# Two inner loops swapped around the 32 small matmuls that form a chunk's state increments

## The chip, the cores and the metric

The kernel runs on one core of one Trainium2 chip. The metric is the device time of one execution in microseconds (us), as the median of several runs. The profile is of one further execution.

## What is computed

A gated linear recurrence over the sequence, per batch and head, followed by a two-layer network with a PReLU between the layers. Everything is float32.

```python
B, H, S, D = 4, 8, 768, 48
f = sigmoid(f_logit)
for t in range(S):
    state = f[:, :, t, :, None] * state + outer(k[:, :, t], v[:, :, t])   # per batch, head: D x D
    y[:, :, t] = q[:, :, t] @ state
x = y.transpose(0, 2, 1, 3).reshape(B * S, H * D)      # 3072 x 384
h = x @ w_in                                            # 384 x 2048
out = (maximum(h, 0) + alpha * minimum(h, 0)) @ w_out   # 2048 x 384
```

## The kernel before

The sequence is cut into 6 chunks of `C = 128` positions, and each chunk into `NC2 = 2` halves of `CH = 64`. Two batches (`U = 2`) are worked on together, so that there are 12 steps: for each chunk, first batches 0 and 1 (`bp = 0`), then 2 and 3 (`bp = 1`). The 8 heads stand as `HP = 4` pairs: the 48 dims of the even head of a pair (`par = 0`) on partitions 0 to 47, those of the odd head (`par = 1`) on 64 to 111. A tile that is named by its dims holds key or query dims on partitions and time along the row.

Each step has three parts, written as generators:

- `prepare` loads f, q, k and v of the chunk (`L223`, `L233`) and forms on VectorE (DVE) and ScalarE (ACT) the decayed queries and keys: products of gates within groups of four positions, scans over blocks of 32, and from these `q3`, `ks`, `kh` and `f64` (the decay over one half).
- `attend` runs the matmuls of the recurrence: `raw` (`L343`) and `qu` (`L359`) give the scores within blocks of 32 positions, `off` (`L377`) those between the two blocks of a half. `pk` (`L390`) turns the decayed keys `ks` so that time lies on partitions, and ACT copies them to `ksn` (`L393`). Then `pd` (`L406`) forms the increments of the state; this is the place of the change. `moved` (`L416` to `L421`, DVE) adds an increment to the decayed state, and `py` (`L434`) forms the outputs from state, scores and v.
- `network` runs the two layers over the 256 rows of the step: `ph` (`L464`), PReLU on ACT and DVE (`L469`, `L472`), `po` (`L480`), and the results leave from `o` (`L486`).

The increments. For batch `u`, head `2 hp + par` and half `cc`, the increment is the product of the half's decayed keys (64 positions x 64 columns, of which 48 are dims) with its values (64 positions x 48). The positions of half 0 lie on partitions 0 to 63 and those of half 1 on 64 to 127, both in `ksn` and in `vs`; so this decides the rows of TensorE's 128 x 128 array that a matmul uses. The result of half 0 goes to partitions 0 to 63 of `pd`, and that of half 1 to 64 to 127; this decides the columns. A matmul of half 0 thus uses the quarter of the array with rows and columns 0 to 63, one of half 1 the quarter with rows and columns 64 to 127. `par` and `hp` only choose other columns of the same tiles. `pd` is a pair of banks of the accumulator memory PSUM, one for each `u`. There are U x HP x NC2 x 2 = 32 of these matmuls in a step. In the profile each float32 matmul shows as two loads of its weights (LDWEIGHTS, on "PEld") and two MATMULs (on "PE").

`py` for comparison: its 32 matmuls use all 128 rows, and `par` chooses columns 0 to 63 or 64 to 127 (`L434`); `par` is its innermost loop. In `raw`, `qu` and `off`, `par` is the innermost loop too and there chooses the rows, while the next loop out chooses the columns.

The order on TensorE (PE), DVE and ACT is written by hand. The strings `first` and `usual` (`L496` to `L502`) name the generators to advance, one letter for each: S for `attend`, n for the network of the step before, Q for `prepare` of the next step, P for `prepare` of this one, w and v for the two weight matrices. In a usual step, network matmuls of the step before stand between the stages of `attend`:

```python
usual = "n S n S Q n2 Q S n2 S Q n S Q S Q n5 Q"
```

SyncE, ScalarE and GpSimd (POOL) issue the DMAs; the v of later steps comes through POOL's queue (`L233`).

Of the kernel before, what the change touches and what calls it, by code (L numbers as in the profile page):

```python
# [23 lines left out]
NC2 = C // CH  # L24
# [6 lines left out]
def kernel(  # L31
# [179 lines left out]
    def halves(cc):  # L211

        return slice(CH * cc, CH * cc + CH), slice(CH * (1 - cc), CH * (1 - cc) + D)
# [116 lines left out]
    def attend(bp, c, x):  # L330
# [68 lines left out]
        pd = pair(f"pd_{i}")  # L399
        for u in range(U):  # L400
            for hp in range(HP):
                for cc in range(NC2):
                    for par in range(2):
                        o = (2 * hp + par) * D
                        s_ = halves(cc)[0]
                        nc.tensor.matmul(pd[s_, u, o:o + D],  # L406
                                         lhsT=ksn[s_, u, hp * 128 + 64 * par:hp * 128 + 64 * par + 64],
                                         rhs=vs[bp][s_, cc, u, o:o + D], start=True, stop=True)
# [96 lines left out]
    def begin(n):  # L505
        if n >= len(steps):
            return None, None, None
        x = {}
        return [stage(*steps[n], x) for stage in (prepare, attend, network)]
# [67 lines left out]
```

## Time and profile before

| | |
|---|---|
| three runs | 691.63, 692.16, 692.86 us; median 692.16 |
| the profiled execution | 692.21 us, of which the span (first to last instruction) 690.4 |
| busy over the span | PE 638.1 us (92%), PEld 477.7 (69%), DVE 440.3 (64%), ACT 232.6 (34%), POOL 50.2 (7%) |
| chain that ended last, by engine | PE 73%, DVE 22%, ACT 2% |
| mean granted TensorE clock | 0.988 of full speed |
| `ph` matmuls (`L464`) | 1152 instructions, 267.2 us busy |
| `po` matmuls (`L480`) | 768 instructions, 251.3 us busy |

The profile is of one execution. PE is the matmul itself, PEld the load of weights, which overlaps with PE. "Busy" of an engine is the time in which at least one of its instructions ran, so instructions that overlap are counted once, while "mean ns" is the duration of a single one. The chain is followed back from the last instruction, at each step to what released it. "Idle before" is the time in which the engine stood still just ahead of the group, and what ended most of it. The ends of matmuls are modelled.

### The profile page before, as it was taken

To read this page: it belongs to the slowest core of one execution; us is meant where nothing else is said; L and a number is where in the kernel's file an instruction comes from. 1 tells how busy PE (TensorE), PEld (TensorE's weight loads), DVE (VectorE), ACT (ScalarE), POOL (GpSimd) and SP (SyncE) were. 2 spreads that over 40 slices of the span, in tenths; PEclk is the share of its full clock that TensorE was granted. 3 is DMA by queue.
4 is the path that set the end of the run, shared out by engine and by line. 5 is a ranking of instruction groups with operands and counts; after the bars stand their busy time and mean duration, and the time that the engine had idled before them with its cause. 6 is when DMAs were issued, how large, how long until landed. Compare 5 with 4: busy or idle time off the path is not lost.

```text
span 690.4 us, 16917 instructions
## 1 busy us (share of the span) xinstructions
PE 638.1 (92%) x7392; PEld 477.7 (69%) x7392; DVE 440.3 (64%) x907; ACT 232.6 (34%) x397; POOL 50.2 (7%) x89
## 2 busy tenths in 40 slices
PE   1367699999999999999999999999999999999998
PEld 0256476876876785785785786786786786786774
DVE  6998999996675693593594594495495494340120
ACT  3554573260352340440440440440440440240110
POOL 9010000010000010010010010000000000000000
PEclk9998899999999999999999999999999999999999
DMA  6656545121121220221211211121121000000000
GB/s 234 205 144 184 153 129 163 55 94 47 56 62 47 86 60 19 83 55 26 73 55 37 61 59 43 57 62 46 54 66 46 25 2 24 25 3 24 23 1 23
DMA packets 25673, 46.74 MB, mean 68 GB/s; under 512 B 3936, under 2 KB 16480, under 8 KB 25600
## 3 DMA queue, kind: packets, MB, share of 16 engines
q0 software_dynamic: 6160, 21.63, 10.9%
q1 hardware_dynamic: 13584, 21.63, 9.8%
q10 hardware_dynamic: 5856, 2.40, 1.4%
q8 instruction: 58, 0.95, 0.6%
q14 instruction: 15, 0.12, 0.1%
HBM read 36.21 MB, written 4.72 MB: 59 GB/s over the span
## 4 chain that ended last, share of the span: by engine, by line
PE 73%; DVE 22%; ACT 2%; issue 1%; DMA 1%; DVEq 0%; ACTq 0%; SPq 0%
PE po L480 33%; PE ph L464 28%; DVE ad L364 4%; PE pd L406 3%; DVE ad L350 3%; PE py L434 3%; DVE g L472 2%; PE qu L359 2%; PE pk L390 2%; PE raw L343 2%; DVE us L275 1%; DVE us L262 1%; DVE w_in_sb L189 1%; DVE w_in_sb L186 1%; PE off L377 1%
## 5 line engine op out<-in xcount | busy, mean ns | idle before, releaser
L464 PE MATMUL ph<-xT,w_in_sb 128*128 128x256 f32 x1152 | 267.2, 387 | 7.3 <-DMA xT<-y 7.3
L480 PE MATMUL po<-w_out_sb,g 128*128 128x384 f32 x768 | 251.3, 487 | 0.1
L464 PEld LDWEIGHTS ph<-xT,w_in_sb 128*128 128x128 f32 x1152 | 218.1, 193 | 43.4 <-DMA xT<-y 7.5
L480 PEld LDWEIGHTS po<-w_out_sb,g 128*128 128x128 f32 x768 | 145.3, 190 | 98.7 <-DVE w_out_sb L189 1.1
L472 DVE SCALAR_TENSOR_TENSOR g<-neg,om,ph 128x256 f32<-128x256 f32 x192 | 82.3, 476 | 193.2 <-ACT neg L469 193.0
L469 ACT ACTIVATE neg<-ph 128x512 f32<-128x512 f32 x96 | 56.9, 595 | 191.9 <-PE ph L464 115.9
L486 ACT COPY o<-po 128x384 f32<-128x384 f32 x24 | 11.5, 479 | 179.5 <-PE po L480 179.5
L364 DVE COPY_PREDICATED ad<-mquad,qu 128x224 f32<-128x224 int32 (+6 forms) x168 | 50.5, 300 | 8.0 <-DVE ad L364 0.3
L350 DVE COPY_PREDICATED ad<-mraw,raw 128x256 f32<-128x256 int32 x96 | 42.6, 444 | 11.8 <-PE raw L343 9.1
L359 PE MATMUL qu<-us,k 48*32 48x116 f32 x1536 | 28.8, 285 | 20.0 <-DVE us L275 14.1
L343 PE MATMUL raw<-qd,k 48*32 48x128 f32 x1536 | 29.3, 286 | 16.5 <-DVE qd L244 10.9
L275 DVE TENSOR_TENSOR us<-us,fs 128x768 f32<-128x768 f32 (+2 forms) x72 | 44.2, 613 | 0.1
L359 PEld LDWEIGHTS qu<-us,k 48*32 48x32 f32 x1536 | 23.5, 113 | 23.6 <-DVE us L275 14.8
L343 PEld LDWEIGHTS raw<-qd,k 48*32 48x32 f32 x1536 | 22.6, 110 | 24.4 <-issue 23.8
L326 ACT COPY A<-q 48x512 f32<-48x512 f32 x48 | 29.6, 617 | 10.3 <-DVE q L294 5.5
L397 ACT COPY A<-ad 32x512 f32<-32x512 f32 x48 | 29.5, 615 | 0.6
L406 PEld LDWEIGHTS pd<-vs,ksn 64*64 64x64 f32 x768 | 25.3, 141 | 5.7 <-issue 3.2
L244 DVE TENSOR_TENSOR qd<-qd,f 128x768 f32<-128x768 f32 (+2 forms) x36 | 27.3, 758 | 3.0 <-ACT qd L239 3.0
L434 PEld LDWEIGHTS py<-A,vs 128*64 128x64 f32 x768 | 25.0, 145 | 5.3 <-issue 4.3
L406 PE MATMUL pd<-vs,ksn 64*64 64x48 f32 x768 | 26.8, 227 | 1.2 <-ACT ksn L393 1.2
L434 PE MATMUL py<-A,vs 128*64 128x64 f32 x768 | 26.9, 231 | 0.8 <-DVE vs L416 0.8
L223 POOL DMA_DIRECT2D k<-in_kT x11 | 8.0, 727 | 255.7 <-PE raw L343 255.7
(65 smaller groups left out, 425.3 us busy)
## 6 DMA issues: line engine op xcount, KB each, us to landing
w_in_raw<-in_w_in SPq DMA_DIRECT2D x12, 511.8 KB, 4.6
w_out_raw<-in_w_out SPq DMA_DIRECT2D x12, 511.8 KB, 3.5
f<-in_fT POOLq DMA_DIRECT2D x11, 512.0 KB, 4.1
q<-in_qT POOLq DMA_DIRECT2D x11, 512.0 KB, 4.4
k<-in_kT POOLq DMA_DIRECT2D x11, 512.0 KB, 4.5
out<-o SPq DMA_DIRECT2D x24, 192.0 KB, 1.8
vs<-in_v POOLq DMA_DIRECT2D x22, 192.0 KB, 3.3
xT<-y SPq DMA_DIRECT2D x36, 48.0 KB, 3.0
```

What stands on the lines that cost most here:

```text
L275: nc.vector.tensor_tensor(us[:, :, UO[m]:UO[m] + 4 * n].rearrange("p g (i r) -> p g i r", r=4), us[:, :, skip:skip + 4 * n].rearrange("p g ...
L326: nc.scalar.copy(A[halves(cc)[1], :, par * HP:(par + 1) * HP, CH * cc:CH * (cc + 1)], q3[rows(par)].rearrange("p (u h c) s t -> p u h c (s ...
L343: nc.tensor.matmul(raw[DB * j:DB * (j + 1), par, hp * C:(hp + 1) * C], lhsT=k[r_, g:g + DB], rhs=qd[r_, 0:4 * W].rearrange("p (d x) -> p d ...
L350: nc.vector.copy_predicated(adu, mraw[:, d].rearrange("p i r -> p (i r)").bitcast(I32).unsqueeze(1).broadcast_to((128, H, DB)), rv[:, :, d])
L359: nc.tensor.matmul(qu[DB * j:DB * (j + 1), par, hp * UW:(hp + 1) * UW], lhsT=k4[r_, g * DB:(g + 1) * DB], rhs=us[r_, g], start=True, stop= ...
L364: nc.vector.copy_predicated(ad[:, u, :, :, 4 * m:DB], mquad[:, lo:lo + n].bitcast(I32).unsqueeze(1).unsqueeze(1).broadcast_to((128, 2, HP, ...
L406: nc.tensor.matmul(pd[s_, u, o:o + D], lhsT=ksn[s_, u, hp * 128 + 64 * par:hp * 128 + 64 * par + 64], rhs=vs[bp][s_, cc, u, o:o + D], star ...
L434: nc.tensor.matmul(py[64 * par:64 * par + 64, u, o:o + CH], lhsT=vs[bp][:, cc, u, hd * D:hd * D + 64], rhs=A[:, u, par * HP + hp, CH * cc: ...
L464: nc.tensor.matmul(ph[:, j * T:(j + 1) * T], lhsT=w_in_sb[:, kt, (f + j) * 128:(f + j + 1) * 128], rhs=xT[:, kt], start=(kt == 0), stop=(k ...
L469: nc.scalar.activation(neg, phv, AF.Relu, scale=-1.0)
L472: nc.vector.scalar_tensor_tensor(g[:, j], neg[:, j], om[:, f + j:f + j + 1], phv[:, j], ALU.mult, ALU.add)
L480: nc.tensor.matmul(po[u][:, 0:DM], lhsT=gs[f // 2][:, f % 2, u * C:(u + 1) * C], rhs=w_out_sb[:, f], start=(f == 0), stop=(f == NF - 1))
```

## The change

The loops over `par` and `cc` change places; `cc`, the half, is now the innermost. The body stays: the same 32 products, with the same operands and the same places in `pd`.

```diff
         for u in range(U):
             for hp in range(HP):
-                for cc in range(NC2):
-                    for par in range(2):
+                for par in range(2):
+                    for cc in range(NC2):
                         o = (2 * hp + par) * D
                         s_ = halves(cc)[0]
                         nc.tensor.matmul(pd[s_, u, o:o + D],
```

For each pair of heads the four matmuls came as half 0 even head, half 0 odd head, half 1 even head, half 1 odd head. Now they come as half 0 even, half 1 even, half 0 odd, half 1 odd. In the program of the changed kernel, the wait for the v of half 1 stands at the second matmul of a stage where it stood at the third; the order of the instructions on the other engines is the same.

## The prediction

> **What bounds the kernel now.** I read the page first: busy times, slices, the chain that ended last, the costliest groups. Then busy time by stretch, one stretch for each of the 12 chunk steps, the timeline of one step, and the single instructions of L406. The page, as columns: busy us (share of the span) and instructions; slices in tenths; shares of the chain; then groups with busy us, mean ns of one | idle before.
>
> ```profile
> span 690.4 us, 16917 instructions
> ...
> PE   1367699999999999999999999999999999999998
> ...
> PEclk9998899999999999999999999999999999999999
> ...
> PE po L480 33%; PE ph L464 28%; DVE ad L364 4%; PE pd L406 3%; DVE ad L350 3%; PE py L434 3%; DVE g L472 2%; PE qu L359 2%; PE pk L390 2%; PE raw L343 2%; DVE us L275 1%; DVE us L262 1%; DVE w_in_sb L189 1%; DVE w_in_sb L186 1%; PE off L377 1%
> ...
> L359 PE MATMUL qu<-us,k 48*32 48x116 f32 x1536 | 28.8, 285 | 20.0 <-DVE us L275 14.1
> ...
> L406 PEld LDWEIGHTS pd<-vs,ksn 64*64 64x64 f32 x768 | 25.3, 141 | 5.7 <-issue 3.2
> ...
> L434 PEld LDWEIGHTS py<-A,vs 128*64 128x64 f32 x768 | 25.0, 145 | 5.3 <-issue 4.3
> L406 PE MATMUL pd<-vs,ksn 64*64 64x48 f32 x768 | 26.8, 227 | 1.2 <-ACT ksn L393 1.2
> L434 PE MATMUL py<-A,vs 128*64 128x64 f32 x768 | 26.9, 231 | 0.8 <-DVE vs L416 0.8
> ```
>
> The reader is to see three things. TensorE (PE) is full from about the sixth slice (some 85 us) to the end. The edited line, L406, is on the chain with 3% of the span, so what it gains or loses ends up in the time. And all of L406 is 26.8 us of PE, so nothing done to it can be worth more than that. A matmul of the source shows as two loads and two matmul instructions: 12 steps x 32 matmuls = 384 in the source, 768 in the row.
>
> The steps, as stretches: length, PE busy (count), PEld busy, DVE, ACT, POOL, clock, DMA.
>
> ```profile
> 304.80:357.20 52.40, 51.98 (x618) 38.87 (x617) 33.58 (x69) 16.55 (x29) 3.38 (x5) 1.00 0.19 54
> ```
>
> PE is busy for 51.98 of 52.40 us, VectorE (DVE) for 33.58. What is saved on PE in such a step comes off the step, and the same holds for what is added. The timeline around that step's L406 and L434 (start, us of the group):
>
> ```profile
> 353.29 1.98 PEld L406 LDWEIGHTS pd<-vs,ksn 64*64 64x64 f32 x64 [0.33 <-issue]
> 353.29 2.10 PE L406 MATMUL pd<-vs,ksn 64*64 64x48 f32 x64
> ...
> 355.32 2.46 PEld L464 LDWEIGHTS ph<-xT,w_in_sb 128*128 128x128 f32 x12
> ...
> 358.11 1.95 PEld L434 LDWEIGHTS py<-A,vs 128*64 128x64 f32 x64 [0.33 <-issue]
> 358.11 2.09 PE L434 MATMUL py<-A,vs 128*64 128x64 f32 x64
> ```
>
> So one L406 stage is 64 loads in 1.98 us, 31 ns each, though one load lasts 135 ns from start to end; the work is pipelined, and what counts is the distance between starts.
>
> **The change part by part.** No instruction is added or removed, no shape changes, and no other line moves. Per stage, 32 matmuls change their order. A matmul of half 0 uses rows 0 to 63 and columns 0 to 63 of the array, one of half 1 rows and columns 64 to 127. Before, the halves come as 0 0 1 1; after, 0 1 0 1. The question is whether the two quarters worked one after the other before.
>
> *Do they overlap already?* The records of single instructions in the stage at 353.29 say yes. Loads start at 353.293, .306, .348, .361, .404, .417: pairs 13 ns apart, a new pair every 55 to 58 ns. The second load waits on a semaphore which in the program belongs to the third matmul, the first of half 1 (it waits for that half's v). So the first load of half 1 starts 13 ns after the first of half 0, although three load-and-matmul pairs of half 0 stand between them in program order. Each quarter then runs its own stream at about 58 ns per load, and the stage is 32 loads x 58 ns = 1.86 us plus some 0.12 us of tail: the 1.98 of the view. The streams are side by side already; the order within a run of four decides only by how much half 1 lags. The window view of the first 30 ns agrees (two matmuls and two loads in flight, four matmuls by 120 ns; columns as above, PE and PEld alone):
>
> ```profile
> 353.29:353.32 0.03, 0.03 (x2) 0.03 (x2) 1.00 0.00 0
> ...
> 353.38:353.41 0.03, 0.03 (x4) 0.03 (x5) 1.00 0.00 0
> ```
>
> *The gain.* py (L434) is the trace's own example of the new order: its 32 matmuls of 64-column loads alternate between two column halves at every matmul. Its stage takes 1.95 us of loads against 1.98, and 2.09 against 2.10 of PE. At the end of a stage of the old order (the one at 615.35) the last matmul of half 0 starts at 617.191 and that of half 1 at 617.232, a lag of 41 ns; in py the lag of the pair is 7 ns. Both ways: 41 - 7 = 34 ns, and 1.98 - 1.95 = 0.03 us. Taken as 0.03 us x 12 stages = **0.4 us**, all on PE and so on the path.
>
> *The wait that moves.* The wait for half 1's v moves from the third matmul of a stage to the second, some 13 ns sooner at the queue. Behind it stand the stage's other matmuls, the next ph or po, and DVE's state update L421. It costs nothing: the v loads (L233) are issued right after a py stage (at 360.40 in the timeline) for a later step, and the group of v transfers lands 3.3 us after issue. If that cover were gone, a late landing would already hold the third matmul now, 13 ns later; 12 x 13 ns = 0.16 us is the most.
>
> *Cost not shown: changing quarters twice as often.* A stage changes quarter 15 times before and 31 after: 16 more, 192 in all. No row of the trace has this very order, so I bound a change of quarter. From above: qu changes rows at every matmul, and its 64 instructions take 28.8 us / 24 stages = 1.20 us, 37 ns per matmul with everything included; 192 x 37 ns = 7.1 us is the most a loss can be. From below: L406 falling to qu's rate, (2.10 - 1.20) x 12 = a gain of 10.8 us; but qu loads 32 columns over eight parts of the array, and L406 loads 64 over two, so this end is far. The nearest row is py, with the same load width, two parts and 31 changes: 2.09 us, no loss and 0.01 to 0.03 of gain. I take that value.
>
> [...]
>
> **Sum.** 692.21 (the profiled execution: span 690.4 and 1.8 around it) - 0.4 = 691.8. The median shown, 692.16, stands 0.05 below the profiled one, so 691.8 by either. I call a change of up to 0.2% (1.4 us) no change, about what a measurement of this kernel can tell: its three runs lie between 691.63 and 692.86.
>
> **The rivals.**
> *It does what its words say*: the halves were mostly waiting for each other and now overlap. For it: 31 ns per instruction is well above qu's 19. Against it: the start pairs, and py at the same rate with a finer alternation. It would give 692.2 - 10.8 = 681.4 at qu's rate; a partial one, in which the pitch within a quarter falls from 58 to the 55 ns seen at the start of a stage, gives 32 x 3 ns x 12 = 1.2 us more than the lag, 690.6. Chance of over 0.2% faster: 7%.
> *Changing quarters costs*: a switch in both rows and columns delays the next load. It decides (0.2% slower) from 1.4 us / 192 = 7.3 ns per extra change, on top of the lag's 0.4 us; at 37 ns it gives 692.2 + 7.1 = 699.3, at half of it 695.7. For it: two of L406's neighbours differing in both is what the trace has only 15 times per stage. Against it: the lag between quarters hides a change as long as a stream has queued loads, and qu and raw also step from one pair of row and column groups to another with no gap. Chance: 5%.
> *The two streams lose their overlap* (shared bank or queue): a stage of 2.10 becomes at most 4.2, + 2.1 x 12 = 25 us, 717. Nothing in the trace points to it. Chance: 2%.
>
> **How the numbers follow.** Forecast (no change by the bound, around 691.8): 86%. Faster by over 0.2%: 7%. Slower by over 0.2%: 7% (5 + 2). The forecast alone holds more than 8 in 10, so the range is its own: from 690.5, the partial gain of 1.2 us with the lag, to 693.4, the runs' highest 692.86 with some 3 ns per extra change (0.6 us). The far bounds, 681 and 699, lie in the cases left out.
>
> **What would show it.** In the changed profile one L406 stage should take 1.94 to 1.96 us of loads and 2.06 to 2.10 of PE, a usual step 52.3 to 52.4 us, and starts should come in pairs 7 ns apart. Loads of 1.9 or less mean that the pitch itself fell; 2.1 or more mean that changing quarters costs; 3 and more, that the overlap is lost. I am wrong if the stream in a quarter isn't set by its own 58 ns per load but by what the other quarter does between.

## The result and the profile after

The change made no difference that a measurement of the whole kernel can tell. Four runs gave 692.25 to 693.41 us, median 692.43, beside 692.47 for the kernel before: a ratio of 1.0004, interval 0.9987 to 1.0021. A second comparison with more runs (11 of the changed kernel, 15 of the one before) gave 691.98 beside 692.42, a ratio of 0.9996, interval 0.9987 to 1.0005. The forecast was 691.8 and no change.

The page of the changed kernel (its profiled execution: 692.39 us), the lines that answer to those of before:

```profile
span 690.6 us, 16917 instructions
...
PE po L480 36%; PE ph L464 31%; PE pd L406 4%; PE py L434 3%; DVE ad L364 3%; DVE ad L350 3%; PE qu L359 2%; PE raw L343 2%; PE pk L390 2%; DVE g L472 1%; PE off L377 1%; DVE w_in_sb L189 1%; DVE w_in_sb L186 1%; DVE us L262 1%; DVE us L275 1%
...
L406 PEld LDWEIGHTS pd<-vs,ksn 64*64 64x64 f32 x768 | 24.9, 142 | 5.7 <-issue 3.2
L434 PEld LDWEIGHTS py<-A,vs 128*64 128x64 f32 x768 | 25.0, 145 | 5.3 <-issue 3.7
L434 PE MATMUL py<-A,vs 128*64 128x64 f32 x768 | 26.9, 231 | 0.8 <-DVE vs L416 0.8
L406 PE MATMUL pd<-vs,ksn 64*64 64x48 f32 x768 | 26.4, 226 | 1.1 <-ACT ksn L393 1.1
```

Of these four rows only L406's moved, by 0.4 us: loads from 25.3 to 24.9, matmuls from 26.8 to 26.4. py is where it was. Rows outside the change moved by more: L464's matmuls went from 267.2 to 268.5 us, with a rise of 1.7 between 60 and 110 us, in the opening of the execution. The timeline of one stage (start, us of the group) and the first 30 ns of it (length, PE busy, PEld busy, clock, DMA):

```profile
353.73 1.94 PEld L406 LDWEIGHTS pd<-vs,ksn 64*64 64x64 f32 x64 [0.33 <-issue]
353.74 2.07 PE L406 MATMUL pd<-vs,ksn 64*64 64x48 f32 x64
```

```profile
353.73:353.76 0.03, 0.02 (x2) 0.03 (x2) 1.00 0.00 0
```

1.94 us of loads where before had 1.98, and at the start two loads in flight, as before. The records of single instructions give the stage more finely: from its first load to its last matmul start, and from its first load to the first load of the next line.

| kernel | matmuls in a row on one half | last matmul start, ns | to the next line, ns | step distance, us |
|---|---|---|---|---|
| before | 2 | 1886 | 2033 | 52.41 |
| changed | 1 | 1852 | 1999 | 52.37 |

The last eleven stages agree within 2 ns in each kernel. The saving is 34 ns in each of them and 29 ns in the first (3613 to 3584): 11 x 34 + 29 = 0.40 us. The first stage is slower because the loads of one half stand 107 ns apart there, 58 in the others. The trace has no clock record that early; 107 ns is also the pitch that the run of sixteen below shows once its granted clock falls to 0.50, so a lower clock in the first stage is likely. The other eleven are called the full-clock stages. The step distance (five steps from the stage at 353 us on, divided by 5) fell by 46 ns: 34 of them are the L406 stage itself, and some 17 appear just ahead of the second qu (L359) of a step, with a few ns given back elsewhere. PE's waits for DVE's `ad` at qu fell from 5.8 to 5.0 us over the execution.

Why does the span not show the 0.4 us? The second stage of L406 started at 101.44 us before and at 102.86 in this execution, 1.4 us later, and at 101.53 in another execution of the same changed kernel. The opening, where the weights are loaded and unpacked, differs by more from one execution to the next than the change is worth.

### The profile page after: what moved, and what is told of

It reads as the page before. It is cut to its first block, busy times and chain, and to the rows that moved or that the text cites. A ratio compares the mean times of both kernels' runs of the same rounds, so it can differ in the third digit from the quotient of the medians.

```text
span 690.6 us, 16917 instructions
## 1 busy us (share of the span) xinstructions
PE 638.2 (92%) x7392; PEld 477.8 (69%) x7392; DVE 440.5 (64%) x907; ACT 232.3 (34%) x397; POOL 50.3 (7%) x89
## 4 chain that ended last, share of the span: by engine, by line
PE 81%; DVE 15%; ACT 2%; issue 1%; DMA 1%; DVEq 0%; ACTq 0%
PE po L480 36%; PE ph L464 31%; PE pd L406 4%; PE py L434 3%; DVE ad L364 3%; DVE ad L350 3%; PE qu L359 2%; PE raw L343 2%; PE pk L390 2%; DVE g L472 1%; PE off L377 1%; DVE w_in_sb L189 1%; DVE w_in_sb L186 1%; DVE us L262 1%; DVE us L275 1%
## 5 line engine op out<-in xcount | busy, mean ns | idle before, releaser
L464 PE MATMUL ph<-xT,w_in_sb 128*128 128x256 f32 x1152 | 268.5, 389 | 7.6 <-DMA xT<-y 7.6
L464 PEld LDWEIGHTS ph<-xT,w_in_sb 128*128 128x128 f32 x1152 | 219.0, 194 | 44.0 <-DMA xT<-y 7.8
L359 PE MATMUL qu<-us,k 48*32 48x116 f32 x1536 | 28.1, 279 | 18.5 <-DVE us L275 13.2
L343 PEld LDWEIGHTS raw<-qd,k 48*32 48x32 f32 x1536 | 22.6, 110 | 25.8 <-issue 24.9
L359 PEld LDWEIGHTS qu<-us,k 48*32 48x32 f32 x1536 | 23.0, 111 | 22.2 <-DVE us L275 13.9
L406 PEld LDWEIGHTS pd<-vs,ksn 64*64 64x64 f32 x768 | 24.9, 142 | 5.7 <-issue 3.2
L434 PE MATMUL py<-A,vs 128*64 128x64 f32 x768 | 26.9, 231 | 0.8 <-DVE vs L416 0.8
L406 PE MATMUL pd<-vs,ksn 64*64 64x48 f32 x768 | 26.4, 226 | 1.1 <-ACT ksn L393 1.1
```

The costliest lines, as they stand in the source:

```text
L343: nc.tensor.matmul(raw[DB * j:DB * (j + 1), par, hp * C:(hp + 1) * C], lhsT=k[r_, g:g + DB], rhs=qd[r_, 0:4 * W].rearrange("p (d x) -> p d ...
L359: nc.tensor.matmul(qu[DB * j:DB * (j + 1), par, hp * UW:(hp + 1) * UW], lhsT=k4[r_, g * DB:(g + 1) * DB], rhs=us[r_, g], start=True, stop= ...
L406: nc.tensor.matmul(pd[s_, u, o:o + D], lhsT=ksn[s_, u, hp * 128 + 64 * par:hp * 128 + 64 * par + 64], rhs=vs[bp][s_, cc, u, o:o + D], star ...
L434: nc.tensor.matmul(py[64 * par:64 * par + 64, u, o:o + CH], lhsT=vs[bp][:, cc, u, hd * D:hd * D + 64], rhs=A[:, u, par * HP + hp, CH * cc: ...
L464: nc.tensor.matmul(ph[:, j * T:(j + 1) * T], lhsT=w_in_sb[:, kt, (f + j) * 128:(f + j + 1) * 128], rhs=xT[:, kt], start=(kt == 0), stop=(k ...
```

## The experiments

**Theory.** Each of the two quarters of TensorE's array works on a stream of its own. Its pitch, measured at 58.3 ns, is set by the load of 64 columns, and the other quarter plays no part. I take it that the instructions are handed out in program order, and that the front can run only some way ahead of a quarter that is busy; no record shows the handing out itself. In the old order half 1's fifth pair (a pair is one load with its matmul) started late: its load came 274 ns after the stage's first, 4 ns after half 0's fifth matmul had begun. The first four pairs of half 1 lag by 13 ns, those from the fifth on by 41 to 47. From that I read a rule, an estimate that the runs below are to test: a pair is handed out when the matmul three places before it in the same quarter has started. With 58.3 ns and 3.3 ns of issue per pair (an estimate from the 13 ns that the first four pairs of half 0 put ahead of half 1's first) this rule gives 1853 ns for the new order and 1893 for the old; the measured 1852 and 1886 fit, but the rule was read from them. **Rivals:** each change of quarter has a price; the order never matters; the two quarters share one stream of 29 ns per pair.

### Runs of four

```diff
-            for hp in range(HP):
+            for h2 in range(0, HP, 2):
                 for cc in range(NC2):
-                    for par in range(2):
+                    for hp, par in ((h2, 0), (h2, 1), (h2 + 1, 0), (h2 + 1, 1)):
```

> Four matmuls of half 0 follow each other, then four of half 1 (the old order has two, the changed one has one). Theory: each quarter of the array has a stream of its own with a load every 58.3 ns, and TensorE's front, which hands out matmuls in program order, can run ahead in one quarter by about three load-and-matmul pairs beyond the one that is matmulling; so longer runs starve the other quarter. Worked through for 58.3 ns and three pairs ahead, the last start lies 1.85 us after the first for runs of one, 1.89 for runs of two (measured 1.85 and 1.89), and 2.40 for runs of four. So the stage, from its first load to the next line's first load, goes from 2.03 us of before to about 2.55, + 0.52 x 12 = 6 us and some more in the first, slow-clock stage: about 699. Rival 1 (each change of quarter has a price): half as many changes, so the stage gets shorter than 2.03 and the time stays or falls below 692. Rival 2 (the order never matters, look-ahead is deep enough): 2.03 us and 692.

Measured: 697.69 us (one run; before 692.27 on the same chip). The stage near 356 us in the timeline:

```profile
355.89 2.46 PEld L406 LDWEIGHTS pd<-vs,ksn 64*64 64x64 f32 x64 [0.33 <-issue]
355.89 2.58 PE L406 MATMUL pd<-vs,ksn 64*64 64x48 f32 x64
```

Last start 2364 ns, 2511 to the next line: 0.48 us more per stage, 11 x 0.48 + 0.67 in the first = 5.9, and the span grew by 5.5. The theory's 2.40 us was 0.04 too long, and the time is 1.3 us under the expected 699. Fewer changes of quarter made the stage longer, so a price per change is not what sets it; and the order does matter with runs of four, 2511 ns where runs of two had 2033 (by the rule a run of four is eight pairs, well beyond the look-ahead; the old order's run of two, four pairs, is one pair beyond it and cost the lag of 34 ns). Both of the first two rivals fall.

### Runs of sixteen

```diff
-        for u in range(U):
-            for hp in range(HP):
-                for cc in range(NC2):
+        for cc in range(NC2):
+            for u in range(U):
+                for hp in range(HP):
                     for par in range(2):
```

> All 16 matmuls of half 0, then all 16 of half 1. Theory (three pairs of look-ahead): the streams run one after the other but for the few pairs ahead, last start 3.52 us after the first, stage about 3.66 us, + 1.63 x 12 = 20 us and some 1.6 more in the slow-clock first stage: about 713. Rival 1 (price per change of quarter): one change per stage in place of 15, so below 692. Rival 2 (look-ahead of 32 pairs or more, TensorE taking whatever quarter is free): 692. This is also the price of a lost overlap, which the prediction put at 25 us at most.

Measured: 719.08 us (one run). The stage in the timeline:

```profile
366.98 3.61 PEld L406 LDWEIGHTS pd<-vs,ksn 64*64 64x64 f32 x64 [0.33 <-issue]
366.98 3.73 PE L406 MATMUL pd<-vs,ksn 64*64 64x48 f32 x64
...
370.76 0.95 DVE L421 TENSOR_TENSOR vs<-vs,pd 48x768 f32<-48x768 f32 x1 [1.13 <-PE pd L406]
```

64 loads in 3.61 us, 56 ns each: one stream after the other. The last matmul start lies 3519 or 3520 ns after the first load in nine of the eleven full-clock stages, where the theory said 3.52 us; the estimate of three pairs of look-ahead fits a kernel it was not read from. DVE's state update now waits 1.13 us for pd, which the old order did not show.

The time is 6 us over the expected 713. Summed over the twelve stages, the longer L406 is worth 21.3 us of the 26.9 by which the span grew. More than half of the rest comes with the clock. The rows below are three pairs of stretches: each time 3.41 us that lie almost wholly in an L406 stage, then the 3.41 us behind them (length, PE, PEld, DVE, ACT, POOL, clock, DMA):

```profile
106.46:109.87 3.41, 3.41 (x62) 3.36 (x61) 3.31 (x8) 2.28 (x4) 0.00 (x0) 1.00 0.77 249
109.87:113.28 3.41, 3.41 (x6) 1.90 (x7) 3.31 (x8) 1.58 (x3) 0.00 (x0) 0.50 0.79 214
475.10:478.51 3.41, 3.41 (x64) 3.41 (x63) 1.97 (x4) 0.60 (x1) 0.36 (x1) 1.00 0.55 154
478.51:481.92 3.41, 3.41 (x12) 2.76 (x11) 2.97 (x4) 0.00 (x0) 0.00 (x0) 0.50 0.00 0
638.94:642.35 3.41, 3.41 (x62) 3.39 (x62) 2.18 (x4) 0.60 (x1) 0.00 (x0) 1.00 0.02 5
642.35:645.76 3.41, 3.41 (x13) 2.78 (x12) 0.95 (x1) 0.00 (x0) 0.00 (x0) 0.50 0.01 2
```

PE is shown busy all through, and still the granted clock fell to 0.50 for 3.41 us. Behind the stage at 475.04 the twelve `ph` matmuls took 4.36 us where they take 2.86 at full clock, and in the last stage, where the fall comes before its end, the pitch goes from 58 to 107 ns. Beyond the longer L406, the steps with the two late falls are 1.7 and 1.4 us longer than before, the step with the early one 0.9, and the opening ahead of it 1.6; between the two executions of the changed kernel above the opening differed by 1.3 us without any such cause.

Which three stages of the eleven? The falls start at 109.87, 478.51 and 642.35 us, and the distances are 108 and 48 times 3.413 us, so they lie on one grid (in the profile of before, too, the changes of the granted clock lie 1, 2 and 4 times that apart: 3.41, 6.83 and 13.65 us). On that grid the stretch just before the fall lay inside the stage for 95, 100 and 99% of its length. In the eight stages without a fall no stretch of the grid was covered by more than 87%. That is read from one execution; what made the clock fall was not shown.

### Half 1 with 4 pairs in place of 32

```diff
         for u in range(U):
+            s_ = halves(1)[0]
+            nc.tensor.matmul(pd[s_, u, 0:DM], lhsT=ksn[s_, u, 0:64],
+                             rhs=vs[bp][s_, 1, u, 0:DM], start=True, stop=True)
             for hp in range(HP):
                 for par in range(2):
-                    for cc in range(NC2):
+                    for cc in range(1):
```

> Leaves out the increments of half 1: in their place one matmul per batch with wrong operands fills that part of pd (64 columns loaded, 384 moving), so half 1 has 4 load-and-matmul pairs in a stage where it had 32. Half 0 is as before. Theory (a quarter's own stream of 32 x 58.3 ns sets the stage, the other quarter is free): 28 of 64 pairs less and still a stage of about 1.99 to 2.00 us, as in the changed kernel; time 692. Rival (the two quarters share one stream, 29 ns per pair whoever it is for): 28 x 29 ns = 0.81 us less per stage, 1.19 us, and 692 - 9.7 = 682.

Measured: 693.25 us (one run; 692.27 for before). In its numbering L409 is half 0, L402 the four wide pairs of half 1 per stage:

```profile
L409 PE MATMUL pd<-vs,ksn 64*64 64x48 f32 x384 | 26.3, 226 | 0.0
L409 PEld LDWEIGHTS pd<-vs,ksn 64*64 64x64 f32 x384 | 24.8, 142 | 0.0
```

Half the instructions, and the same busy time: 24.8 us of loads for 384, where the changed kernel has 24.9 for 768. The stage is 1998 ns, the changed kernel's own 1999. Half 0's stream took as long with 4 pairs beside it as with 32; the rival of one shared stream (682 us) falls. Half 1 isn't idle in this run: its four wide matmuls move as many columns as the 32 small ones (4 x 384 = 32 x 48). But half 0's matmuls start 58 or 59 ns apart both beside them and in the last 0.25 us of the stage, when they are done. So the old order's stage, 2033 ns, stood only the lag of 34 ns above what half 0's own stream takes.

### Loads of 48 columns, in both orders

The load carries 64 columns, of which 16 are padding.

```diff
-                        nc.tensor.matmul(pd[s_, u, o:o + D],
-                                         lhsT=ksn[s_, u, hp * 128 + 64 * par:hp * 128 + 64 * par + 64],
+                        nc.tensor.matmul(pd[CH * cc:CH * cc + D, u, o:o + D],
+                                         lhsT=ksn[s_, u, hp * 128 + 64 * par:hp * 128 + 64 * par + D],
```

> The changed order, and each increment loads only the 48 columns that hold dims where it loaded 64 (the 16 others are padding); the moving side keeps its 48 columns. Theory (the pitch of 58.3 ns within a quarter is the load of 64 columns: py with 64 moving columns and pd with 48 have the same pitch, and at half clock it is 107 ns): the pitch falls by a quarter of 53 ns to about 45 ns, the stage from 2.00 to 1.57 us, 0.43 x 12 = 5 us, time 687. Rival (58 ns is a fixed handling time per pair, or is set by the array's 64-column part whatever is loaded): stage 2.00, time 692.

> Loads of 48 columns with the old order (0 0 1 1). Theory: the pitch within a quarter is that of the run with 48 columns and the new order, 45 ns, and the half 1 stream lags as it does with 64 columns; worked through with a look-ahead of three pairs, the last start lies 1.48 us after the first against the 1.44 measured with the new order: 0.04 us per stage, 0.5 us per execution, time 687.7 where the new order had 687.25. Rival (with shorter loads the handing out in program order becomes the limit, and the order decides more): last start 1.6 us or later, 2 us or more per execution, 689 and above.

Measured with the new order: 687.25 us, ratio 0.9929, interval 0.9913 to 0.9946. With the old order: 687.32 us, ratio 0.9930, interval 0.9915 to 0.9946. The new order's stage and its row:

```profile
350.81 1.52 PEld L406 LDWEIGHTS pd<-vs,ksn 64*48 64x48 f32 x64 [0.33 <-issue]
350.81 1.64 PE L406 MATMUL pd<-vs,ksn 64*48 64x48 f32 x64
```

```profile
L406 PEld LDWEIGHTS pd<-vs,ksn 64*48 64x48 f32 x768 | 19.3, 127 | 5.7 <-issue 3.2
```

The pitch fell from 58.3 to 45 ns (starts 7 and 38 ns apart in turn), the stage from 1999 to 1572 ns: 11 x 0.427 + 0.85 in the first = 5.5 us, and the span fell by 5.4. So the width of the load set the pitch here: 16 columns fewer took 13.3 ns off it. The old order's stage (length of the stretch, PE, PEld, clock, DMA):

```profile
350.10:351.90 1.80, 1.68 (x64) 1.55 (x64) 1.00 0.32 36
```

It is 1606 ns to the next line, its last start at 1473 where the new order has 1438: a lag of 35 ns, close to the 34 with 64 columns; expected were 40. The time does not tell the two orders apart; the stages do.

### Narrow loads in py too

```diff
-                        nc.tensor.matmul(py[64 * par:64 * par + 64, u, o:o + CH],
-                                         lhsT=vs[bp][:, cc, u, hd * D:hd * D + 64],
+                        nc.tensor.matmul(py[rows(par), u, o:o + CH],
+                                         lhsT=vs[bp][:, cc, u, hd * D:hd * D + D],
...
-            nc.scalar.copy(y[:, u].rearrange("p h t -> p (h t)"), py[:, u])
+            for par in range(2):
+                nc.scalar.copy(y[rows(par), u].rearrange("p h t -> p (h t)"), py[rows(par), u])
```

> New order and 48-column loads in the increments, and 48-column loads in the output matmuls py as well (its copies to y are cut in two, one for each half of the partitions, 12 x 2 more copies on ScalarE). py moves 64 columns per matmul, the increments 48. Theory (a quarter's pitch is the longer of its load and its moving columns, each of 64 taking 53 ns, plus 5): py keeps 58 ns, its stage stays 2.02 us, and the time stays at 687.3, or a little above if a copy comes late. Rival (the load alone sets the pitch): py's stage falls by 0.43 us, 12 x 0.43 = 5.1, time 682.

Measured: 689.84 us, ratio 0.9961, interval 0.9948 to 0.9975: 2.6 us more than without this step.

```profile
L434 PEld LDWEIGHTS py<-A,vs 128*48 128x48 f32 x768 | 23.9, 129 | 5.4 <-issue 4.8
L434 PE MATMUL py<-A,vs 128*48 128x64 f32 x768 | 25.9, 228 | 0.8 <-DVE vs L416 0.8
```

py fell only from 25.0 to 23.9 us of loads (with its 64 moving columns the stage went from 2015 to 1924 ns, pitch 58 to 56), where the rival of the load alone wanted 5 us. So in py something else than the load holds the pitch at 56 ns, where the increments with the same load had 45. Their 48 moving columns against py's 64 fit; py's matmuls also use all 128 rows where the increments use 64, and no run separates the two. The theory was near, 0.09 us per stage off: it had 58 ns, measured were 56. Later steps did get shorter, by 0.09 us, to 51.86; the loss comes at the start. The second L406 stage began at 103.56 us in the profiled execution where the kernel without this step had 101.21. In the first step the copies to `y` took 2.37 us where two whole ones had taken 1.07, PE's wait for the transfers `xT<-y` behind them was 8.76 us where it was 7.83, and ScalarE was busy for 247.4 us in all where it had 232.3. That the 24 extra copies also delay the unpacking of weights on ScalarE in the opening is likely; no run took it apart.

### The changed kernel once more

> The changed kernel once more, with more rounds. Theory: 0.034 us per stage less, 0.4 us in all, a ratio of 0.9994 that its interval will hardly tell from 1; the stage is 2.00 us from its first load to the next line's first load in each of the eleven full-clock stages, against 2.03. Rival (something outside the stage takes the 0.4 us back): the later steps, of stages three to twelve, come at the same distance as before, 52.41 us, where theory has 52.37.

Measured: 691.98 us, ratio 0.9996, as told above. The stage near 353 us (length, PE, PEld, clock, DMA):

```profile
352.90:355.10 2.20, 2.07 (x64) 1.94 (x64) 1.00 0.41 74
```

1998 to 2000 ns to the next line in all eleven stages, and a step distance of 52.37 us. Nothing gives the gain back; it is 0.4 us of 692.

## Why the prediction was right

- *TensorE is full, so L406 counts in full*: right, as far as the opening lets one see. In runs4, half a microsecond added per stage came through to the span (5.9 added, 5.5 seen), and in cols48 5.4 came off for 5.5 saved.
- *The halves overlap already; each runs its own stream at 58 ns*: right, and the centre of it. With 4 pairs in place of 32 in half 1 the stage did not get shorter; with the overlap really taken away (runs16) it grew to 3.67 us.
- *The gain is the lag, 0.03 us x 12 = 0.4 us*: right in place and size: 34 ns x 11 + 29. py as the example of the new order gave 1.95 and 2.09 us; measured were 1.94 and 2.07. Where the lag comes from the prediction did not say: it took the size from the end of a stage, and the look-ahead of three pairs that fits the starts was read from them afterwards. In the whole kernel's time the 0.4 us itself is not shown, since both intervals take in no change.
- *The moved wait costs nothing*: right; the idle time before L406's loads stayed 5.7 us.
- *Changing quarters, from -10.8 to +7.1 us, taken as nothing*: right. runs4, with half as many changes, was slower.
- *The partial gain, pitch from 58 to 55 ns*: did not come. In this stage only a narrower load moved the pitch, from 58.3 to 45 ns with 48 columns for 64.
- *Lost overlap "at most 4.2 us", 717*: this term was mis-sized. The stage is 3.67 us at full clock, shorter than the bound, and the longer L406 is worth 21.3 us where the bound had 25. But the time was 719.08, over it: 5.6 us came outside L406, 3.1 of them in the steps of the two late clock falls. The bound had taken for granted that the clock stays and the rest of the kernel keeps its time.
- *A shared bank or queue*, which the prediction names with that rival: no delay from a shared bank shows in the changed kernel, where the two halves write different partitions of one bank at starts 7 ns apart. Starts were out of program order between quarters: before the change, half 1's first load came 13 ns after half 0's first, ahead of three pairs that stand before it in the program.
- *The 53 ns for 64 columns*, in the expectations for narrower loads: no run shows this term by itself. The runs showed 13.3 ns less pitch for 16 columns fewer (58.3 to 45), which by proportion is an estimate of 53 for 64, and a pitch of 107 ns, twice 53.5, in the stretches with the clock at 0.50.

## What to carry to other kernels

Before reordering matmuls so that they fall on different parts of the array, look whether they overlap already: compare the stage's time with one part's own stream (32 x 58 ns here), not with the number of instructions. Runs of two matmuls on one part cost only the lag here, 34 ns per stage, while runs of four and sixteen cost 0.5 and 1.7 us. In the run of sixteen, where work stayed mostly in one quarter at a time for 3.7 us, the granted clock also fell to 0.50 for 3.41 us behind three of eleven stages. What shortened this stage was a narrower load: leaving 16 columns of padding out of it took 0.7% off the kernel.

## What the runs showed of the hardware that was not expected

- A quarter that was free started late behind one that was busy: half 1's last matmul came 1886 ns after the stage's first load with runs of two, 2364 with four, 3519 with sixteen, and 1852 with alternating halves. The estimate of about three pairs of look-ahead, with the pitch of 58.3 ns, gave 1.89, 2.40 and 3.52 us.
- The pitch of a load-and-matmul pair in a quarter was 58.3 ns with 64 loaded and 48 moving columns, 45 with 48 and 48, and in py's column halves 58 with 64 and 64, 56 with 48 loaded and 64 moving.
- The granted clock fell to 0.50 for 3.41 us with PE busy throughout, behind three of the eleven 3.7 us stages of runs16 in which mostly one quarter worked at a time. These three covered 95, 100 and 99% of the stretch before the fall, on the 3.41 us grid on which the falls lie; the other eight covered at most 87% of any stretch and had no fall.
